# A re-ordered opening in a fused sliding-window attention and tanh-shrink layer

## The chip, the cores and the metric

The kernel runs on one core of one Trainium2 chip. The metric is the device time of one launch in microseconds (us), the median of three runs. Engine names are those of the profile: PE (TensorE matmuls), PEld (its weight loads), DVE (VectorE), ACT (ScalarE), POOL (GpSimd) and SP (SyncE, which here only issues transfers).

## The reference

Eight batches of eight heads, 576 tokens of 64 numbers. Each token attends to itself and the 63 tokens before it. The result, 4608 tokens of 512 numbers, goes through two matrix products with a tanh shrink between them.

```python
scores = scale * np.matmul(q, k.transpose(0, 1, 3, 2))
mask = (rel >= 0) & (rel < 64)              # rel = query position - key position
scores = np.where(mask, scores, -1e9)
attn = np.exp(scores - scores.max(-1, keepdims=True)); attn /= attn.sum(-1, keepdims=True)
x = np.matmul(attn, v).transpose(0, 2, 1, 3).reshape(4608, 512)
h = x @ w_in                                # 512 -> 2048
out = (h - np.tanh(h)) @ w_out              # 2048 -> 512
```

## The kernel before

The whole program is a list of some 1170 short words, `PLAN`, that `play` reads from left to right. Each word issues a handful of instructions, and every engine runs its own instructions strictly in the order of the list; between engines semaphores hold an instruction back until its operands are ready. So the list alone sets who is queued behind whom, on each engine and on the two queues that issue transfers, POOL's and SP's.

Attention goes by *pairs* of heads (four pairs in a batch, so pair 9 is the second of batch 2). The words for a pair g, with the engine:

- `lk`/`lq` load k and q (POOL, which casts float32 to bfloat16 on the way; the two with `.s` go through SP in float32). `ck`/`cq` re-arrange the loaded rows on the engine named by the last letter (p POOL, a ACT, v DVE). The first pairs are transposed without that step.
- `Ep`/`Fp` transpose q and k on PE, `Ec`/`Fc` copy the result out of PSUM (ACT or DVE).
- `Rp` computes the scores of half a pair on PE, `Rx` the exponentials on ACT. For pairs 0 to 3 the mask is added by a matmul of `hide`; from pair 4 on DVE multiplies by a mask (`M`).
- `LV.b.i` loads one tile of 128 tokens of v of batch b, `lv` and `lt` parts of batch 1; `zr`, `za`, `zb`, `Z` copy v to the other half of the partitions. A pair's product with v needs all five tiles of its batch and their copies.
- `P` (pairs 0 to 3) and `PP` (two pairs at once) compute probabilities times v on PE; `D`, `DS`+`DH` and `DR`+`DN` divide by the row sums on DVE. P.0, P.1 and P.3 use the same two PSUM banks, so each waits for the division of the one before.
- `Xp` transposes the attention result on PE, `Xc` copies it into a chunk of 512 tokens (`xT`).

The layers go by chunks c of 512 tokens and blocks m of 128 of the 2048 hidden numbers: `H.c.m` is four matmuls of 512 columns with w_in, `Hp.c.m.half` two of them, for one half of the input (half 0 comes from the first two pairs of the batch). `A` is the tanh on ACT, `G` the subtraction on DVE; for the first two chunks the results rotate through three PSUM banks. `W.c.s.part` is four matmuls with the part-th quarter of w_out, `O` copies the finished 128 tokens out of PSUM and SP stores them. `wi` and `wo` load the five blocks of w_in and the four of w_out. `U.n.bank` issues n matmuls of a constant tile whose result nobody reads.

From batch 3 on, rows of k and q are loaded by token (`lr`, `qr`) and transposed by SP's transfers (`tk`, `tq`); `S` computes the scores of two pairs there and needs all of the batch's transposed q and k.

Two rules of the queues matter below. POOL works in order, its own copies (`cq.4.p` and the like) and fills among its transfers, and its transfers rotate through eight semaphores, so that one is issued only when the eighth before it has landed. SP issues transposing transfers and the stores of the output from one queue.

Of the kernel before, what the change touches and what calls it, by code (L numbers as in the profile page):

```python
# [15 lines left out]
def kernel(  # L16
# [9 lines left out]
    nc = tc.nc  # L26
    B, H, S, D = q.shape
    NP = H // 2
    NJ = S // 64
    E, P = 6, S // 6  # L30
# [7 lines left out]
    M = d_ff // 128  # L38
# [162 lines left out]
    def make_ident():  # L201
        nc.gpsimd.memset(ident, 0.0)
# [312 lines left out]
    def subtract(c, m, s=None):  # L515
# [3 lines left out]
        i=make_ident, u=make_warm, mv=pads_v, mt=pads_k, mk=pads_kw, mz=pads_q8, tz=tail_q, U=warm_up, h=make_hide, n=make_mask, N=put_mask,  # L519
# [12 lines left out]
    def play(script):  # L532
# [5 lines left out]
        u mv.0 mv.1 lk.1.p lq.2.p LV.0.2 U.1.3 U.1.3 U.1.5 U.1.7 U.1.6 lk.3.p U.1.1 U.1.7 lk.2.p U.1.7 lq.1.p  # L538
        lq.3.p U.4.3 LV.0.0 i lk.0.s lq.0.s U.1.3 U.1.2 U.4.0 LV.0.3 U.4.0 Ep.2.3 Fp.1.5 U.1.2 Ec.2.3.v zr.0.2.v
        Fc.1.5.a ck.0.a mt.3 mt.1 U.1.1 U.1.3 U.1.2 U.1.4 mt.2 U.1.1 U.1.4 cq.0.a Fp.0.1 Fp.2.6 Ep.0.2 LV.0.1  # L540
        Ep.1.3 U.1.7 Fp.3.5 Fc.2.6.a LV.0.4 lk.4.p lq.4.p h Ec.0.2.a Fc.3.5.a Ep.3.7 Ec.3.7.a Ec.1.3.v mt.0
        Fc.0.1.v Rp.1.0.3 lk.5.p Rp.3.0.1 Rx.1.0.3 Rp.0.1.5 zr.0.3.v Rx.3.0.1 zr.0.0.v zr.0.1.v Rp.1.1.4
        Rp.3.1.0 ck.4.v Rx.0.1.5 Rx.1.1.4 Rx.3.1.0 lq.5.p Rp.0.0.2 wi.1 wi.0 lq.6.p P.1 lv.1.1.0 lk.7.p D.1
        Rx.0.0.2 cq.4.v Rp.2.1.0 Rp.2.0.3 Rx.2.1.0 P.0 Rx.2.0.3 P.2 Fp.4.2 ck.5.a Fc.4.2.a D.0 Ep.4.4 DS.2 P.3
        U.1.3 lk.6.p DH.2.0 Ec.4.4.a wi.2 Xp.0.0.1.2 Fp.5.0 Xp.0.0.0.3 D.3 lv.1.0.1 lk.8.p lq.7.p U.1.4 DH.2.1
        Xc.0.0.0.3.v Rp.4.1.5 U.1.1 lv.1.1.1 Xc.0.0.1.2.v Xp.0.1.0.7 cq.5.a Xp.0.1.1.1 Ep.5.3 Fc.5.0.a
        Xc.0.1.1.1.v Rx.4.1.5 Hp.0.0.0 mz Xc.0.1.0.7.a ck.7.a Ec.5.3.v Hp.0.2.1 Hp.0.0.1 Rp.4.0.6 Rp.5.1.3 n
        Hp.0.1.0 U.1.5 Hp.0.2.0 Hp.0.1.1 cq.6.v ck.6.v A.0.0 Ep.6.5 Rx.5.1.3 Rx.4.0.6 G.0.0 lv.1.0.0 A.0.2 A.0.1
        G.0.2 wi.3 H.0.3 A.0.3 G.0.1 N U.1.7 G.0.3 lq.8.p Fp.6.3 cq.7.v Fp.7.7 Ec.6.5.a H.0.4 ck.8.a H.0.6
# [101 lines left out]
```

## Time and profile before

| | us |
|---|---|
| median of three runs | 307.73 (307.4 to 307.78) |
| the profiled execution, first to last instruction | 305.2 |
| PE busy | 297.8 |
| the first layer's first matmul starts (Hp.0.0.0) | 22.58 |
| first matmul of W.2.0.1, from where both plans are alike | 109.08 |

The profiled execution's own span is 305.2 us; 2.5 us of the median lie outside it. Times in the profile count from the first instruction. A row of the timeline gives the start, the duration, the engine, the line of the kernel, the operation with its operands, and how often it stands there in a row; in brackets stands how long the engine was idle before it, and what ended the wait. A matmul's row ends some 0.2 us after the next matmul may start, so paces are read from start to start.

### The profile page before, as it was taken

What the parts mean: (1) busy time and instruction counts of PE and PEld (TensorE: products, weight loads), DVE (VectorE), ACT (ScalarE), POOL (GpSimd) and SP (SyncE); (2) the same over time, 40 slices, a digit from 0 to 9 for tenths busy, and PEclk for the clock granted to TensorE, in tenths of its full rate; (3) what the DMA queues carried; (4) which work ended last, traced back from release to release, by engine and by line L of the source; (5) the groups of instructions that cost most, each with busy time, mean ns of one, the idle gap of its engine ahead of it and who ended that gap; (6) DMA issues with size and microseconds to landing.
All of it is one profiled execution on the core that took longest, in us unless ns stands there. A gap on an engine that the chain in (4) does not pass through costs nothing.

```text
span 305.2 us, 6469 instructions
## 1 busy us (share of the span) xinstructions
PE 297.8 (98%) x2599; PEld 149.4 (49%) x2632; DVE 176.2 (58%) x316; ACT 157.5 (52%) x265; POOL 103.7 (34%) x141
## 2 busy tenths in 40 slices
PE   8999999999999999999999999999999999999995
PEld 3574555545455545444544444444544444444443
DVE  1687993289577745675387475657673645355300
ACT  1898975487565346534564645345633433433211
POOL 8989775800994290019005770000000000000000
PEclk9999999999999999999999999999999999999999
DMA  9999999995999999949999999560143010001112
GB/s 155 159 195 193 195 207 180 159 205 102 102 143 127 173 125 181 182 108 131 164 177 127 135 173 142 95 143 35 37 76 74 0 69 37 34 34 37 52 51 104
DMA packets 132878, 36.77 MB, mean 120 GB/s; under 512 B 119920, under 2 KB 127344, under 8 KB 132848
## 3 DMA queue, kind: packets, MB, share of 16 engines
q0 software_dynamic: 92752, 18.06, 85.3%
q1 hardware_dynamic: 40096, 18.30, 31.5%
q8 instruction: 20, 0.33, 0.5%
q14 instruction: 10, 0.08, 0.1%
HBM read 36.70 MB, written 9.44 MB: 151 GB/s over the span
## 4 chain that ended last, share of the span: by engine, by line
PE 87%; DVE 5%; ACT 3%; issue 2%; POOL 2%; DVEq 0%; ACTq 0%; POOLq 0%
PE ps L474 38%; PE ps L431 30%; PE ps L508 6%; PE ps L348 3%; PE ps L304 2%; DVE gT L445 2%; PE ps L397 1%; ACT th L439 1%; PE ps L286 1%; PE ps L467 1%; DVE pt L323 1%; PE ps L260 1%; PE ps L281 1%; PE ps L227 1%; POOL qall L110 1%
## 5 line engine op out<-in xcount | busy, mean ns | idle before, releaser
L445 DVE TENSOR_TENSOR gT<-ps,th 128x512 bf16<-128x512 f32 x144 | 97.2, 687 | 85.3 <-ACT th L439 84.6
L474 PE MATMUL ps<-w_out_sb,gT 128*128 128x512 bf16 x527 | 131.5, 380 | 2.2 <-issue 0.8
L439 ACT ACTIVATE th<-ps 128x512 f32<-128x512 f32 x144 | 84.7, 599 | 93.0 <-PE ps L431 79.7
L431 PE MATMUL ps<-xT,wi 128*128 128x512 bf16 x496 | 120.7, 380 | 0.1
L474 PEld LDWEIGHTS <-gT 128*128 128x128 bf16 x560 | 53.3, 98 | 61.4
L431 PEld LDWEIGHTS <-wi 128*128 128x128 bf16 x496 | 47.0, 98 | 54.3
L145 POOL DMA_DIRECT2D vw<-in_v_dram x35 | 30.0, 872 | 36.1 <-PE ps L348 33.5
L90 ACT ACTIVATE ysb<-ps 128x512 f32<-128x512 f32 (+1 forms) x24 | 14.2, 593 | 30.9 <-PE ps L474 30.2
L166 POOL DMA_DIRECT2D qall<-in_q_dram x25 | 21.7, 881 | 24.1 <-DMA qw<-qall 21.4
L166 POOL DMA_DIRECT2D kall<-in_k_dram x25 | 21.7, 875 | 10.4 <-DMA kw<-kall 4.8
L314 ACT ACTIVATE pt<-ps 128x1024 bf16<-128x1024 f32 (+1 forms) x30 | 23.3, 816 | 3.5 <-PE ps L304 3.2
L323 DVE TENSOR_TENSOR pt<-pt,ps 128x1152 bf16<-128x1152 bf16 x28 | 20.5, 749 | 5.1 <-ACT pt L314 3.2
L508 PE MATMUL ps<-xT,wi 128*128 128x512 bf16 x80 | 20.8, 380 | 0.0
L92 DVE COPY ysb<-ps 128x512 f32<-128x512 f32 (+1 forms) x11 | 7.1, 650 | 20.5 <-PE ps L467 13.2
L368 DVE TENSOR_TENSOR xs<-ps,rcp 128x384 bf16<-128x384 f32 x28 | 15.2, 550 | 0.3
L318 ACT ACTIVATE pt<-ps 128x640 bf16<-128x640 f32 (+1 forms) x24 | 14.7, 659 | 0.8 <-PE ps L286 0.8
L348 PEld LDWEIGHTS <-pt 128*64 128x64 bf16 x504 | 9.4, 112 | 6.3 <-DVE pt L323 2.1
L90 ACT ACTIVATE kt<-ps 128x576 bf16<-128x576 bf16 x10 | 6.5, 647 | 10.8 <-PE ps L256 6.8
L227 PE MATMUL ps<-warm 128*128 128x512 bf16 (+1 forms) x35 | 10.6, 435 | 1.1 <-DVE warm L207 1.1
L508 PEld LDWEIGHTS <-wi 128*128 128x128 bf16 x80 | 7.4, 98 | 8.5 <-issue 0.4
L348 PE MATMUL ps<-vw,pt 128*64 128x65 bf16 x504 | 11.0, 197 | 0.3 <-DVE pt L323 0.2
L365 DVE TENSOR_TENSOR xs<-ps,rcp 128x384 bf16<-128x384 f32 x14 | 7.7, 550 | 0.1
(74 smaller groups left out, 166.7 us busy)
## 6 DMA issues: line engine op xcount, KB each, us to landing
out_dram<-ysb SPq DMA_DIRECT2D x33, 256.0 KB, 3.1
vw<-in_v_dram POOLq DMA_DIRECT2D x28, 128.0 KB, 6.6
qall<-in_q_dram POOLq DMA_DIRECT2D x20, 128.0 KB, 7.5
kall<-in_k_dram POOLq DMA_DIRECT2D x20, 128.0 KB, 6.8
w_out_sb<-in_moe_w_out_dram POOLq DMA_DIRECT2D x4, 512.0 KB, 8.2
kall<-in_k_dram POOLq DMA_DIRECT2D x11, 144.0 KB, 6.3
qall<-in_q_dram POOLq DMA_DIRECT2D x11, 144.0 KB, 6.6
wi<-in_moe_w_in_dram POOLq DMA_DIRECT2D x3, 512.0 KB, 7.9
```

Of the source, the lines that this page charges most:

```text
L90: nc.scalar.activation(o, i, ACT.Copy)
L145: nc.gpsimd.dma_start(out=w[:, 2 * i + 1, :, 0:D] if i < NF else w[64:128, 2 * i, :, 0:D], in_=v[b, :, 128 * i:128 * i + n].rearrange("h p ...
L166: nc.gpsimd.dma_start(out=token_rows(b, n)[0:c, i], in_=(q if n == "q" else k)[b, :, 128 * i:128 * i + c].rearrange("h p d -> p h d"))
L314: nc.scalar.activation(o, sp, ACT.Exp, scale=scale)
L323: nc.vector.tensor_tensor(p, p, mask.unsqueeze(1).to_broadcast([128, 2 * NJ, 64]), ALU.mult)
L348: nc.tensor.matmul(ps[r, bank, 65 * i:65 * i + 65], PT[(g + r2) % NPT][:, j, r], vw[b % 2][:, j, p0 + r2 + NP * h, :], start=True, stop=True)
L368: nc.vector.tensor_tensor(xs[b % 2][:, p0 // 2, 0:6, n // 2, :], ov[:, :, 0:D], sums[g][:, n].to_broadcast([128, 6, D]), ALU.mult)
L431: nc.tensor.matmul(hp, w_in_tile(ki, m), chunk_tile(c)[:, n.start // 64:n.stop // 64, ki % 2, 64 * (ki // 2):64 * (ki // 2) + 64], start=( ...
L439: nc.scalar.activation(th[:, n], hp, ACT.Tanh)
L445: nc.vector.tensor_tensor(gT[c][:, m, columns(s)], hp, th, ALU.subtract)
L474: nc.tensor.matmul(yp, gT[c][:, m, s * 128:(s + 1) * 128], w_out_sb[:, m, :], start=n == 1 and i == 0, stop=n == 4 and i == 3)
L508: nc.tensor.matmul(hp, w_in_tile(half + 2 * i, m), chunk_tile(c)[:, :, half, 64 * i:64 * i + 64], start=n == 1 and i == 0, stop=n == 2 and ...
```

## The change

Three things change in the code, and the first 550 words of the plan (570 before); the last 604 words are the same.

- The three constant tiles `ident`, `hide` and `seen` are filled by DVE in a new word `iv`; POOL keeps only the selects.
- Copies out of PSUM, casts and copies of v change engines here and there: k of pair 0 is cast by DVE (`ck.0.v`), q of pair 4 and k of pairs 5, 8 and 9 by POOL (`cq.4.p`, `ck.5.p`, `ck.9.p`, `ck.8.p`).
- The order: q of pairs 2, 0 and 1 is transposed first; three of w_out's four blocks are issued close together; k and q of batch 2 are loaded behind w_out, and batch 3's loads and transposes stand in one piece. There are 30 matmuls of the constant tile in place of 35.

```diff
     def make_ident():
-        nc.gpsimd.memset(ident, 0.0)
         nc.gpsimd.affine_select(ident, ident, compare_op=ALU.not_equal, fill=1.0,
                                 base=0, pattern=[[-1, 128]], channel_multiplier=1)
+
+    def fill_masks():
+        nc.vector.memset(ident, 0.0)
+        nc.vector.memset(hide, 0.0)
+        nc.vector.memset(seen, 1.0)
...
     def make_hide():
-        nc.gpsimd.memset(hide, 0.0)
...
     def make_mask():
-        nc.gpsimd.memset(seen, 1.0)
...
-        u mv.0 mv.1 lk.1.p lq.2.p LV.0.2 U.1.3 U.1.3 U.1.5 U.1.7 U.1.6 lk.3.p U.1.1 U.1.7 lk.2.p U.1.7 lq.1.p
-        lq.3.p U.4.3 LV.0.0 i lk.0.s lq.0.s U.1.3 U.1.2 U.4.0 LV.0.3 U.4.0 Ep.2.3 Fp.1.5 U.1.2 Ec.2.3.v zr.0.2.v
...
+        u U.8.3 U.7.4 U.7.2 mv.0 lk.1.p lq.1.p mv.1 lq.0.s cq.0.a lk.0.s mt.0 iv ck.0.v mt.2 lq.2.p LV.0.3 i
+        lk.2.p LV.0.0 lk.3.p LV.0.1 LV.0.2 lk.6.p lq.3.p h LV.0.4 lq.6.p lk.4.p lq.5.p lk.5.p lq.4.p n wi.1 wi.0
+        Ep.2.2 Ep.0.0 Ec.0.0.a Ep.1.1 Ec.1.1.a Ec.2.2.a Fp.0.4 Fp.1.5 U.4.7 Fp.2.3 Fc.1.5.a Fc.0.4.v Rp.0.0.6
...
```

**POOL's first transfers.** `vw_85` is v of batch 0, `kall`/`qall` with 102 and 104 are batch 0 and with 103 and 105 batch 1. Before:

```order
L110 DMA kall_104<-in_k_dram 96x2x384
L110 DMA qall_102<-in_q_dram 96x2x384
L145 DMA vw_85<-in_v_dram 128x8x64
L110 DMA kall_104<-in_k_dram 96x2x384 x2
L110 DMA qall_102<-in_q_dram 96x2x384 x2
L145 DMA vw_85<-in_v_dram 128x8x64
L202 MEMSET ident 128x128
L203 ISA
L203 AFFINE_SELECT ident<-ident 128x128
L145 DMA vw_85<-in_v_dram 128x8x64 x2
L145 DMA vw_85<-in_v_dram 64x8x64
```

Now:

```order
L110 DMA kall_104<-in_k_dram 96x2x384
L110 DMA qall_102<-in_q_dram 96x2x384 x2
L145 DMA vw_85<-in_v_dram 128x8x64
L202 ISA
L202 AFFINE_SELECT ident<-ident 128x128
L110 DMA kall_104<-in_k_dram 96x2x384
L145 DMA vw_85<-in_v_dram 128x8x64
L110 DMA kall_104<-in_k_dram 96x2x384
L145 DMA vw_85<-in_v_dram 128x8x64 x2
L110 DMA kall_105<-in_k_dram 96x2x384
L110 DMA qall_102<-in_q_dram 96x2x384
L234 AFFINE_SELECT hide<-hide 128x128
```

The q of pair 2 goes from second to third place, the q of pair 3 (the last `qall_102`) from seventh to eleventh, and the last, shorter tile of v (64x8x64) from eleventh to twelfth, behind the selects of `hide`.

**ACT ahead of the first layer.** `pt` are exponentials (`Rx`), `qp`/`kt` copied transposes, `xT` the chunks, `th` the tanh. Before, from the sixth of the eight exponentials of pairs 0 to 3 on:

```order
L318 ACTIVATE pt<-ps 128x640
L318 ACTIVATE pt<-ps 128x512
L318 ACTIVATE pt<-ps 128x640
L90 ACTIVATE kb_111<-kall_105 96x2x6x64
L90 ACTIVATE kt_88<-ps 128x576
L90 ACTIVATE qp_94<-ps 128x576
L90 ACTIVATE qb_108<-qall_103 96x2x6x64
L90 ACTIVATE kt_89<-ps 128x576
L318 ACTIVATE pt<-ps 128x512
L90 ACTIVATE xT_112<-ps 128x4x128
L90 ACTIVATE kb_110<-kall_105 96x2x6x64
L439 ACTIVATE th<-ps 128x512
```

Now, from the fifth on:

```order
L320 ACTIVATE pt<-ps 128x512
L90 ACTIVATE qp_97<-ps 128x576
L320 ACTIVATE pt<-ps 128x640 x2
L90 ACTIVATE qb_108<-qall_103 96x2x6x64
L320 ACTIVATE pt<-ps 128x512
L90 ACTIVATE kt_88<-ps 128x576
L90 ACTIVATE xT_112<-ps 128x4x128
L90 ACTIVATE xT_113<-ps 128x128
L90 ACTIVATE qp_96<-ps 128x576
L90 ACTIVATE xT_112<-ps 128x4x128 x2
L90 ACTIVATE xT_113<-ps 128x128
L90 ACTIVATE qp_95<-ps 128x576
```

The cast of pair 5's q (`qb_108`) now stands before the last exponential of pair 3 (the `pt` of 512), and three of the four `Xc` are ACT's.

**SP ahead of batch 4's scores.** `kw_92` and `qw_98` are the transposed k and q of batch 4. Before:

```order
L171 DMA_TRANSPOSE kw_92<-kall_104 128x4x64
L495 DMA out_dram<-ysb 128x512 x2
L171 DMA_TRANSPOSE kw_92<-kall_104 128x4x128
L179 DMA_TRANSPOSE qw_98<-qall_102 128x4x128
L171 DMA_TRANSPOSE kw_92<-kall_104 128x4x128 x2
L179 DMA_TRANSPOSE qw_98<-qall_102 128x4x64
L179 DMA_TRANSPOSE qw_98<-qall_102 128x4x128
L171 DMA_TRANSPOSE kw_92<-kall_104 128x4x128
L179 DMA_TRANSPOSE qw_98<-qall_102 128x4x128 x2
```

Now:

```order
L497 DMA out_dram<-ysb 128x512 x3
L179 DMA_TRANSPOSE qw_98<-qall_102 128x4x128 x2
L171 DMA_TRANSPOSE kw_92<-kall_104 128x4x64
L179 DMA_TRANSPOSE qw_98<-qall_102 128x4x128 x2
L171 DMA_TRANSPOSE kw_92<-kall_104 128x4x128 x3
L179 DMA_TRANSPOSE qw_98<-qall_102 128x4x64
L171 DMA_TRANSPOSE kw_92<-kall_104 128x4x128
```

All ten transposes of batch 4 now stand behind the store of O.1.2; before, one stood ahead of the stores of O.1.0 and O.1.1, and nine between these and the store of O.1.2.

More of the change, by code (lines that the diff above doesn't have):

```diff
@@ new lines @@
+        Hp.2.1.0 A.2.1 O.1.1.v G.2.1 H.2.4 A.2.4 G.2.4 Z.3 S.12 Sx.12.0 Sx.12.2 Sx.12.1 H.2.5 H.2.2 W.1.2.0
+        W.1.2.2 M.12 M.13 A.2.5 A.2.2 PP.12 G.2.2 G.2.5 H.2.10 H.2.7 W.1.2.1 W.1.2.3 A.2.10 A.2.7 DR.12 DN.12.2
+        DN.12.1 G.2.7 DN.12.0 O.1.2.v G.2.10 H.2.9 S.14 A.2.9 H.2.8 Sx.14.0 Sx.14.2 A.2.8 Sx.14.1 G.2.9 G.2.8
+        M.15 M.14 LV.4.3 lr.5.2 qr.5.4 qr.4.4 lr.4.0 LV.4.4 qr.5.3 LV.4.0 lr.5.0 tq.4.2 tq.4.1 tk.4.4 tq.4.0
+        tq.4.3 tk.4.1 tk.4.2 tk.4.3 tq.4.4 tk.4.0 H.2.11 A.2.11 W.1.3.3 W.1.3.1 H.2.12 PP.14 G.2.11 DR.14
@@ new lines @@
+        A.3.13 LV.5.1 LV.5.2 lr.6.1 qr.6.1 A.3.14 G.3.13 W.3.0.2 H.3.15 tz.5.v G.3.14 qr.6.3 H.3.12 W.3.0.0
+        A.3.15 G.3.15 Hp.4.1.0 A.3.12 G.3.12 Hp.4.1.1 A.4.1 W.3.0.1 G.4.1 W.3.0.3 Hp.4.0.1 H.4.3 Hp.4.0.0
+        O.3.0.v tk.6.3 tk.6.2 A.4.0 S.20 A.4.3 Sx.20.2 Sx.20.0 Sx.20.1 tq.6.0 tk.6.0 W.3.1.1 G.4.0 G.4.3 W.3.1.0
+        H.4.2 W.3.1.3 A.4.2 S.22 G.4.2 H.4.4 W.3.1.2 H.4.7 A.4.4 G.4.4 M.20 O.3.1.a Sx.22.0 Sx.22.1 A.4.7
+        W.3.2.1 H.4.6 W.3.2.2 A.4.6 Sx.22.2 W.3.2.3 Z.5 G.4.7 M.22 M.21 H.4.9 PP.20 G.4.6 tq.7.1 tq.6.1 A.4.9
@@ L621 @@
+        H.8.10 A.8.10 G.8.5 G.8.10 W.7.1.3 H.8.9 H.8.8 A.8.9 O.7.1.v A.8.8 W.7.2.3 W.7.2.2 G.8.9 G.8.8 H.8.12
+        H.8.13 A.8.12 A.8.13 W.7.2.1 W.7.2.0 G.8.12 G.8.13 H.8.11 O.7.2.a H.8.14 W.7.3.1 A.8.11 A.8.14 G.8.11
+        H.8.15 W.7.3.3 W.7.3.2 W.7.3.0 A.8.15 G.8.15 G.8.14 W.8.0.3 W.8.0.1 W.8.0.0 O.7.3.v W.8.3.3 W.8.1.3
+        W.8.0.2 W.8.1.2 O.8.0.a W.8.2.2 W.8.1.1 W.8.1.0 W.8.2.3 W.8.2.0 W.8.2.1 O.8.1.a W.8.3.2 O.8.2.a O.9.0.a
+        W.8.3.0 W.8.3.1 O.8.3.v"""
     play(PLAN)
```

147 lines of the change are left out of this document (65 added, 82 removed).

## The prediction

> **What bounds the kernel now.** I read the page first, then PE's busy time by stage, then the timelines of the first 23 us engine by engine.
>
> ```profile
> span 305.2 us, 6469 instructions
> PE 297.8 (98%) x2599; PEld 149.4 (49%) x2632; DVE 176.2 (58%) x316; ACT 157.5 (52%) x265; POOL 103.7 (34%) x141
> PE 87%; DVE 5%; ACT 3%; issue 2%; POOL 2%; DVEq 0%; ACTq 0%; POOLq 0%
> ...
> 0.00:22.58 22.58, 21.07 (x336) 12.42 (x337) 12.17 (x35) 14.43 (x23) 19.50 (x35) 1.00 1.46 169
> 22.58:41.12 18.54, 18.52 (x207) 9.48 (x205) 16.01 (x34) 16.48 (x31) 14.17 (x23) 1.00 1.44 196
> ...
> 90.14:109.08 18.94, 18.59 (x191) 9.77 (x194) 14.37 (x26) 8.09 (x14) 9.73 (x13) 1.00 2.03 145
> ```
>
> PE bounds it: 98% busy, 87% of the chain of waits. The stage rows (stretch, length, then PE, PEld, DVE, ACT, POOL busy, the granted clock, DMA) show that behind 22.58, where the first layer starts, PE is idle for 0.02 us of the next 18.5 and 0.35 of the last 19 before 109. Little is to be had there. What can be gained lies ahead of the first layer, where PE is busy largely with matmuls of the constant tile:
>
> ```profile
> 1.06 6.54 PE L227 MATMUL ps<-warm 128*128 128x512 bf16 x22 [1.06 <-DVE warm L207]
> 7.70 0.45 PE L256 MATMUL ps<-ident,qall 96*64 96x96 bf16 x12
> ...
> 12.46 0.45 PE L281 MATMUL ps<-hide,ident 128*128 128x320 bf16 x2
> ...
> 13.13 0.43 PE L281 MATMUL ps<-hide,ident 128*128 128x320 bf16 x2
> ...
> 16.06 0.51 PE L335 MATMUL ps<-vw,pt 128*64 128x65 bf16 x20
> ...
> 17.81 0.51 PE L335 MATMUL ps<-vw,pt 128*64 128x65 bf16 x20
> ...
> 19.59 0.51 PE L335 MATMUL ps<-vw,pt 128*64 128x65 bf16 x20
> ...
> 22.58 1.54 PE L508 MATMUL ps<-xT,wi 128*128 128x512 bf16 x6
> ...
> 109.08 1.03 PE L474 MATMUL ps<-w_out_sb,gT 128*128 128x512 bf16 x4
> ```
>
> The opening is a chain: load, transpose (7.70), scores (half a pair every 0.67 from 12.46 to 13.13), P.1 (16.06), P.0 (17.81), P.3 (19.59), the division, Xp and Xc, Hp.0.0.0 (22.58). From 109.08 (W.2.0.1) both plans are word for word the same, so **the change is worth the difference in when PE reaches W.2.0.1**, unless a queue arrives there in another state.
>
> Counted by words, PE does the same between the first layer's start and W.2.0.1 in both plans (40 H, 16 Hp, 32 W, six PP, eleven Xp, two S and the scores), but for two things: one group of six transposes more stands ahead of the first layer now, and two single constant matmuls, of 512 and 384 columns, that stood behind it are gone. So the new time of W.2.0.1 is the new start of the first layer, plus the old 86.50 us (109.08 - 22.58), less these two, plus or minus waits.
>
> **The change part by part.** First the loads, since the new chain hangs on them.
>
> ```profile
> 1.36 0.76 POOL L110 DMA_DIRECT2D kall<-in_k_dram  x1 [0.84 <-POOLq L635]
> 2.12 0.65 POOL L110 DMA_DIRECT2D qall<-in_q_dram  x1
> 2.75 0.91 POOL L145 DMA_DIRECT2D vw<-in_v_dram  x1
> ...
> 4.90 1.29 POOL L110 DMA_DIRECT2D qall<-in_q_dram  x2
> ...
> 7.02 0.27 POOL L202 MEMSET ident<- 128x128 bf16 x1
> ...
> qall<-in_q_dram POOLq DMA_DIRECT2D x2, 144.0 KB, 5.4
> ...
> qall<-in_q_dram POOLq DMA_DIRECT2D x2, 144.0 KB, 5.7
> ...
> 13.30 1.41 DVE L92 COPY vw<-vw 64x520 bf16<-64x520 bf16 x4 [0.22 <-DMA vw<-in_v_dram]
> 15.04 0.59 DVE L92 COPY vw<-vw 64x520 bf16<-64x520 bf16 x2 [0.33 <-DMA vw<-in_v_dram]
> ```
>
> The two qall rows are transfers in windows 2 to 5 and 5 to 8 us; their last column is issue to landing. In the second place q landed at 2.12 + 5.4 = 7.5; pair 3's q, seventh, at 5.54 + 5.7 = 11.2; the last full tile of v, tenth, when DVE's wait ends at 15.04. From 11.2 to 15.0 three tiles of v landed, 1.25 us each; between 7.5 and 11.2 one tile and four k or q, so some 0.6 us each for these. By these paces q of pair 2, now third, lands at 8.1 to 8.5 (not 7.5); then tile, k, tile, k, two tiles, k, q: **pair 3's q at 15.5** (11.2 before) and the last, half tile of v at 16.1. The fills that POOL gives up save 0.27 us ahead of this, about what `hide`'s selects now cost ahead of the half tile; on DVE they lie in its idle time before the first copy. I take 0 for them; without that cover they cost the same 0.3.
>
> Step 1, the first transposes: at 8.4 in place of 7.70. The 22 constant matmuls end at 7.6 as before, so PE idles 0.8 us; nothing on the chain waits for it, because step 2 comes later.
>
> Step 2, products with v. The half tile (16.1) sets P.0: the copies of the other tiles (0.59 each) are done by 15.6, pair 3's q is transposed from 15.5 to 15.9. P.0 starts at 16.2 (P.1 before: 16.06). The next product on these banks follows 1.75 later (17.81 - 16.06), as the division needs: P.1 at 17.95.
>
> Step 3, P.3. Prices:
>
> ```profile
> 16.68 0.22 DVE L375 RECIPROCAL rc<-ps 128x10 f32<-128x10 f32 x1 [0.56 <-PE ps L335]
> 16.94 0.82 DVE L377 TENSOR_TENSOR xs<-ps,rc 128x640 bf16<-128x640 f32 x1
> ...
> 13.37 3.50 ACT L318 ACTIVATE pt<-ps 128x640 bf16<-128x640 f32 x6
> ...
> 20.52 0.84 ACT L90 ACTIVATE qb<-qall 96x768 bf16<-96x768 bf16 x1
> ...
> 22.26 0.60 ACT L90 ACTIVATE xT<-ps 128x512 bf16<-128x512 bf16 x1
> ```
>
> Behind P.0 (some 0.45) PE does two halves of scores (0.67 each), pair 2's and pair 3's, to 18.0; pair 3's other half stands behind P.1 (18.4 to 19.1). ACT meanwhile does pair 3's first exponential (from 18.05, 3.50/6 = 0.6), then the cast of pair 5's q (0.84) and only then the last exponential (0.6): 18.05 + 2.05 = 20.1. P.3 starts at 20.1, against 19.59: **+0.5**.
>
> Step 4, into the first layer. P.3 to its division 0.62 (16.68 - 16.06), reciprocal and product 1.1, the last half division 0.4 (half of 0.82), nine transposes on PE 0.5, the last copy on ACT 0.6, and some 0.15 for hand-overs: 20.1 + 3.3 = **23.4 for H.0.3**. The old plan began at 22.58 with Hp.0.0.0, which needs the first two pairs alone; H.0.3 needs all four. So **+0.82**.
>
> Step 5, what was moved ahead of it.
>
> ```profile
> 60.04 0.42 PE L260 MATMUL ps<-ident,kb 96*128 96x96 bf16 x6
> 60.30 0.42 PE L260 MATMUL ps<-ident,qb 96*128 96x96 bf16 x6
> ...
> 285.44 5.18 PE ps L474 x24
> ```
>
> A group of six transposes is 0.26 (60.30 - 60.04). A matmul of 512 columns is 5.18/24 = 0.216, one of 384 three quarters of it, 0.16; the two constant matmuls are 0.38. **-0.64** together. The other constant matmuls stand where PE waits anyway, in both plans.
>
> Step 6, waits behind the start. One goes: DVE copied batch 2's v just ahead of PP.8,
>
> ```profile
> 63.30 2.75 PE L431 MATMUL ps<-xT,wi 128*128 128x512 bf16 x12
> ...
> 65.36 0.71 DVE vw L152
> 66.11 0.76 PE ps L348 x34
> ```
>
> so that PE began it at 66.11 and not at 63.30 + 12 x 0.216 = 65.89. That copy (`Z.2`) now stands some 6 us of PE's work ahead of PP.8: **-0.2**. Others come. A first-layer block holds its PSUM bank for 1.03 on PE (109.08's row has the same four matmuls), about 0.6 on ACT and 0.7 on DVE, 2.35 in all; three banks at 0.864 give 2.59. Each of the seven exponentials (0.6) of this stage exceeds the 0.24 of slack by 0.36, and a group of scores or half a block on PE hides most of it: between 0 and 2.5 in all. I take **+0.55**, near the lower end, because the old plan, with seven such exponentials there too, shows 0.02 us of idle PE in that stage.
>
> The w_in blocks are issued from 15.0 to 18.0 and the fifth behind POOL's cast of pair 4's q. Nearest row for that cast:
>
> ```profile
> 30.73 0.64 POOL L92 COPY vw<-vw 64x520 bf16<-64x520 bf16 x1
> ...
> wi<-in_moe_w_in_dram POOLq DMA_DIRECT2D x1, 512.0 KB, 8.2
> ```
>
> 768 columns by that pace are 0.95. Pair 4's q, fifth behind the half tile, lands at 16.1 + 5 x 0.6 = 19.1, so the cast ends at 20.1, wanted by PE at 22.8. The fifth block lands at 20.1 + 0.8 + 8.2 = 29.1, or 31 behind three others, wanted at 33. The cover is 2 us in both. The w_out blocks stand close together, but the last lands some 2.4 us earlier than before, since two k and two q were put behind it (4 x 0.6). Batch 2's eight k and q and a tile of v then take 8 x 0.6 + 1.25 = 6 us, while PE has ten W (8.6 us) between the first use of that block and the transposes of pairs 10 and 11. These I cost at nothing; without the cover each transfer late is a wait of 0.6 or 1.25.
>
> The sum: +0.82 - 0.64 - 0.2 + 0.55 = **+0.53**, against the profiled span 305.2: 305.7. With the 2.5 us by which the median exceeds the span (307.73 - 305.2), **308.2**.
>
> **The rivals.**
>
> *The opening isn't late.* If the last tile, half as long, lands at 15.3 and P.3's exponential isn't held up, the first layer starts at 22.9; and if the first-layer stage runs like the old one, the 0.55 goes too: +0.3 - 0.64 - 0.2 = -0.5, and without the visible idle time of the last stage row (0.35) -0.9: **306.8**. For it: PE's waits behind 22.58 are few in the old plan, and w_in comes earlier. Against it: four more transfers stand ahead of pair 3's q.
>
> *Casts at the head of in-order engines.* Pair 5's q, third behind the half tile, lands at 17.9 and is wanted by ACT at 18.65; pair 4's k, second, at 17.3, and is wanted by DVE at 17.9. If the loads run 1.5 us late (the three tiles took 1.25 each, a w_in block 8.2 to land), both casts hold up everything behind them: ACT's exponential, DVE's second division. From 0.7 us of lateness on, each further us goes into P.3, and the wait spreads to the first layer's tanh: the forecast's 0.5, 0.8 more in P.3 and 0.7 in the tanh make +2.0, **309.7**.
>
> *The clock.* The rows above show 1.00 granted throughout, also from 7.70 on, where the old plan put seven constant matmuls between the transposes. The new plan has 0.8 us of idle PE there, then transposes with one group of constant matmuls of 384 columns. If the clock fell to half there, the eight groups of scores (0.67 each by 5.4 us in all) would take up to 5.4 more, half of it in the shadow of the loads: +2.7, **310.9**. The Trainium skill, "TensorE: Matmul & The Clock Gate", Part 4, says that transposes don't count as activity for the gate as other matmuls do, and Part 1 that an idle window brings half the clock; by that rule this case would come about, and the trace of before can't tell, having constant matmuls among them.
>
> *Batch 4's transposes.*
>
> ```profile
> 107.15 2.61 SPq L179 DMA_TRANSPOSE qw<-qall  x2
> ...
> 116.27 0.22 PE L299 MATMUL ps<-q,kw 128*128 128x64 bf16 x2
> ...
> kw<-kall SPq DMA_TRANSPOSE x25, 3.9
> ```
>
> SP takes 1.3 each. All ten now stand behind O.1.2's store, at about 98: the last is issued by 111 and lands 3.9 later, at 115, with batch 4's scores due at 116. If the store comes 2 us later, PE waits 1: **309.2**.
>
> *The change does little:* head and waits cancel, **307.7**.
>
> **How the numbers follow.** The forecast 0.37, opening not late 0.27, casts 0.16, clock 0.08, batch 4 0.07, nothing 0.05. About 0.2%, 0.6 us, is what a measurement of this kernel can tell from no change. The forecast's own range is 307.3 to 309.1; of its 0.37 I put 0.17 within 0.2%, 0.17 slower, 0.03 faster. Faster: 0.27 + 0.03 = 0.30. Within 0.2%: 0.17 + 0.05 = 0.22. Slower: 0.17 + 0.16 + 0.08 + 0.07 = 0.48. The range reaches to 306.0 (the first rival, with 0.8 us more) and to 310.8 (the casts with a us more, just short of the clock).
>
> **What would show it.** In the new profile: first transposes at 8.4 (step 1); DVE or PE waiting for vw at 16.1 (step 2); P.3 at 20.1 with ACT's cast right ahead of the last exponential (step 3); H.0.3 at 23.4 (step 4); W.2.0.1 at 109.5. A first layer before 22.9 or after 24.5, a clock below 1.00 in the first 20 us, or PE waiting for wi, w_out or kw/qw would make it wrong.

## The result, and the profile after

The change is slower: 309.17 us (median of 20 runs, 307.74 to 310.13) against 307.92 (20 runs, 307.35 to 309.64), a ratio of 1.0034 with a 95% interval of 1.0019 to 1.0049 (not the quotient of the two medians, which is 1.0041). The forecast was 308.2. The direction is right; the next sections show that a queue which the sum left out has a large part in it.

The page of the changed kernel, with the stage rows of its timeline (stretch, length, then PE, PEld, DVE, ACT, POOL busy, granted clock, DMA):

```profile
span 306.8 us, 6489 instructions
PE 300.0 (98%) x2627; PEld 148.9 (49%) x2627; DVE 182.4 (59%) x323; ACT 150.9 (49%) x256; POOL 107.1 (35%) x143
PE 81%; DMA 9%; POOL 5%; DVE 2%; issue 1%; ACT 1%; SPq 0%; DVEq 0%; POOLq 0%; ACTq 0%
...
0.00:22.80 22.80, 21.14 (x338) 12.19 (x339) 12.94 (x37) 14.57 (x25) 20.87 (x36) 1.00 1.30 164
22.80:41.99 19.19, 18.42 (x187) 8.81 (x187) 13.94 (x25) 14.63 (x28) 12.84 (x20) 1.00 1.35 185
91.01:109.95 18.94, 18.81 (x194) 9.71 (x193) 16.02 (x27) 9.29 (x18) 3.81 (x5) 1.00 1.17 120
```

PE is as busy as before by share, but transfers now have 9% of the chain of waits, where before they had no entry. The stage behind the first layer's start, which had 0.02 us of idle PE, has 0.77. PE's rows that answer to those of the prediction, and all its later waits that the timeline shows:

```profile
1.06 6.57 PE L231 MATMUL ps<-warm 128*128 128x512 bf16 x22 [1.06 <-DVE warm L211]
8.04 0.45 PE L258 MATMUL ps<-ident,qall 96*64 96x96 bf16 x12 [0.40 <-DMA qall<-in_q_dram]
...
15.63 0.49 PE L337 MATMUL ps<-vw,pt 128*64 128x65 bf16 x20
...
19.53 0.51 PE L337 MATMUL ps<-vw,pt 128*64 128x65 bf16 x20
...
22.80 1.02 PE L433 MATMUL ps<-xT,wi 128*128 128x512 bf16 x4
24.53 0.61 PE L510 MATMUL ps<-xT,wi 128*128 128x512 bf16 x2 [0.70 <-DMA wi<-in_moe_w_in_dram]
...
67.57 0.76 PE L350 MATMUL ps<-vw,pt 128*64 128x65 bf16 x36 [0.21 <-DVE qp L92]
68.78 2.87 PE L433 MATMUL ps<-xT,wi 128*128 128x512 bf16 x12 [0.20 <-DVE gT L447]
...
109.95 1.03 PE L476 MATMUL ps<-w_out_sb,gT 128*128 128x512 bf16 x4
...
143.86 0.59 PE L510 MATMUL ps<-xT,wi 128*128 128x512 bf16 x2 [0.44 <-DMA xT<-xs]
```

The first layer starts at 22.80 (22.58 before), W.2.0.1 at 109.95 (109.08). So 0.87 of the 1.6 us between the two profiled spans is there when the common words begin. The other 0.7 comes behind it, in words that are the same in both plans. The wait at 143.86 is Hp.4.1.1's, for the second half of chunk 4's input, which SP's transposing transfers `Y.4.1` bring. The two queues behind it, SP's first, of the kernel before:

```profile
95.58 1.00 SPq L495 DMA_DIRECT2D out_dram<-ysb  x2
96.67 1.31 SPq L171 DMA_TRANSPOSE kw<-kall  x1
...
105.93 3.52 POOL L166 DMA_DIRECT2D kall<-in_k_dram  x4 [4.29 <-DMA qw<-qall]
...
120.90 2.53 SPq L171 DMA_TRANSPOSE kw<-kall  x2
...
135.51 0.53 SPq L495 DMA_DIRECT2D out_dram<-ysb  x1
136.13 2.62 SPq L416 DMA_TRANSPOSE xT<-xs  x2
```

and of the change:

```profile
88.94 10.45 SPq L497 DMA_DIRECT2D out_dram<-ysb  x2
99.48 2.92 SPq L179 DMA_TRANSPOSE qw<-qall  x2
...
112.03 0.88 POOL L166 DMA_DIRECT2D kall<-in_k_dram  x1 [17.21 <-DMA kw<-kall]
...
121.83 3.13 SPq L171 DMA_TRANSPOSE kw<-kall  x2
...
138.09 0.53 SPq L497 DMA_DIRECT2D out_dram<-ysb  x1
138.71 2.63 SPq L418 DMA_TRANSPOSE xT<-xs  x2
```

SP stood from about 89 to 99.4 at the store of O.1.2, which waited for its PE and DVE work, with batch 4's ten transposes queued behind it. The load at the head of POOL's queue, a k tile of batch 6, goes into rows that those transposes read, and loads of batch 5 are queued behind it: POOL stood 17.21 us until 112.03 instead of going on by 105.93. SP's next transposes, of batch 5, read those loads, and the transposes of x stand behind them: they issue at 138.71 in place of 136.13. From the first transposes of batch 5 behind the join (tk.5.2) to those of x, in words that are the same in both plans, SP takes 16.88 us (121.83 to 138.71) in place of 15.23 (120.90 to 136.13). That the late loads cause this is shown only in part: in this execution one of these transposes waits 0.9 us for a load of q, and for SP's other waits the profile names no load. The chain of waits of the change, in order of time, shows the last steps:

```profile
137.61 0.70 DVE gT L447
138.32 0.30 SPq L497
...
138.71 5.11 DMA xT<-xs
143.82 0.04 issue
143.86 0.59 PE ps L510 x2
```

It leads back over the store of O.2.2 (138.32) to DVE, not over POOL's loads, because this store ended SP's last wait; SP had worked off its transposes at 138.00 and stood 0.3 us for the store.

### The profile page after: what moved, and what is told of

Its sections match the earlier page's. It is cut to its first block, busy times and chain, and to the rows that moved or that the text cites. A ratio compares the mean times of both kernels' runs of the same rounds, so it can differ in the third digit from the quotient of the medians.

```text
span 306.8 us, 6489 instructions
## 1 busy us (share of the span) xinstructions
PE 300.0 (98%) x2627; PEld 148.9 (49%) x2627; DVE 182.4 (59%) x323; ACT 150.9 (49%) x256; POOL 107.1 (35%) x143
## 4 chain that ended last, share of the span: by engine, by line
PE 81%; DMA 9%; POOL 5%; DVE 2%; issue 1%; ACT 1%; SPq 0%; DVEq 0%; POOLq 0%; ACTq 0%
PE ps L476 38%; PE ps L433 30%; PE ps L510 5%; DMA wi<-in_moe_w_in_dram 4%; PE ps L350 3%; DMA vw<-in_v_dram 2%; PE ps L306 2%; DMA xT<-xs 2%; DMA qall<-in_q_dram 1%; PE ps L469 1%; PE ps L399 1%; POOL vw L132 1%; POOL vw L145 1%; POOL vw L92 1%; POOL w_out_sb L198 1%
## 5 line engine op out<-in xcount | busy, mean ns | idle before, releaser
L476 PE MATMUL ps<-w_out_sb,gT 128*128 128x512 bf16 x560 | 134.9, 379 | 0.0
L145 POOL DMA_DIRECT2D vw<-in_v_dram x35 | 30.3, 875 | 20.1 <-PE ps L350 16.9
L90 ACT ACTIVATE ysb<-ps 128x512 f32<-128x512 f32 (+1 forms) x20 | 11.8, 592 | 28.4 <-PE ps L476 27.7
L92 DVE COPY ysb<-ps 128x512 f32<-128x512 f32 (+1 forms) x15 | 9.9, 657 | 18.8 <-PE ps L469 13.2
L370 DVE TENSOR_TENSOR xs<-ps,rcp 128x384 bf16<-128x384 f32 x28 | 15.1, 551 | 0.3
L90 ACT ACTIVATE xT<-ps 128x512 bf16<-128x512 bf16 (+3 forms) x15 | 6.6, 491 | 7.7 <-PE ps L399 7.6
L231 PE MATMUL ps<-warm 128*128 128x512 bf16 (+1 forms) x30 | 8.4, 438 | 1.1 <-DVE warm L211 1.1
L92 DVE COPY kt<-ps 128x576 bf16<-128x576 bf16 x8 | 6.0, 749 | 5.2 <-PE ps L262 3.9
```

The source lines that it names most:

```text
L90: nc.scalar.activation(o, i, ACT.Copy)
L92: eng.tensor_copy(o, i)
L145: nc.gpsimd.dma_start(out=w[:, 2 * i + 1, :, 0:D] if i < NF else w[64:128, 2 * i, :, 0:D], in_=v[b, :, 128 * i:128 * i + n].rearrange("h p ...
L476: nc.tensor.matmul(yp, gT[c][:, m, s * 128:(s + 1) * 128], w_out_sb[:, m, :], start=n == 1 and i == 0, stop=n == 4 and i == 3)
```

## The experiments

The ratios are to the kernel before, run beside each kernel on the same chip. The first four kernels share one set of its runs, so do the next four (from the change again to the fills alone) and the last three; the fills' second run has its own.

**Two causes, and the converse.** The first kernel takes away the wait for w_in's block 0; block 4 of chunk 0 is put into the PSUM bank of block 1 before that block is subtracted there, so block 1 of chunk 0 holds other numbers.

```diff
- H.0.3 Hp.0.1.0 A.0.3 ... Hp.0.1.1 N Hp.0.2.0 Rx.6.0.5 A.0.1 G.0.1 Rp.4.0.5 Hp.0.2.1 Rx.4.0.5 A.0.2
+ H.0.3 Hp.0.2.0 A.0.3 ... Hp.0.2.1 N Hp.0.1.0 Rx.6.0.5 A.0.2 G.0.2 Rp.4.0.5 Hp.0.1.1 Rx.4.0.5 A.0.1
```

> The changed kernel, but its second first-layer half block is that of columns 512 to 767 of the first eighth group (Hp.0.2.0, which takes w_in's block 1, landed at 21.4) and the half block that takes w_in's block 0 (landed at 24.5) stands four groups later; no transfer moves. Theory A (0.87 us of the loss is PE's wait for block 0): PE does not wait for wi, W.2.0.1 starts at 109.1 to 109.3 in place of 109.95, ratio to the kernel before 1.0005 to 1.0015 in place of 1.0034. Rival (another chain, tanh or the DVE, takes the place of that wait): W.2.0.1 at 109.7 or later, ratio 1.003.

Measured: 310.17 us, ratio 1.009 (1.0057 to 1.0123). PE no longer waits for wi, yet W.2.0.1 starts at 110.17: a wait of 0.59 for DVE at 30.16 and one of 0.54 ahead of the first layer took the place. Behind the join the wait for x is larger than in the change itself:

```profile
145.48 0.59 PE L510 MATMUL ps<-xT,wi 128*128 128x512 bf16 x2 [1.90 <-DMA xT<-xs]
```

So theory A fails in this form, and the wait for x is not of one size: 0.44 in the change, 1.90 here, with SP's order the same.

The second kernel takes eight of the ten transposes out from behind the store. It is not the old order: the eight now stand together right behind O.1.1's store, and two stay behind O.1.2's.

```diff
- O.1.1.v G.2.1 ... O.1.2.v ... lr.5.0 tq.4.2 tq.4.1 tk.4.4 tq.4.0 tq.4.3 tk.4.1 tk.4.2 tk.4.3 tq.4.4 tk.4.0
+ O.1.1.v tq.4.2 tq.4.1 tk.4.4 tq.4.0 tq.4.3 tk.4.1 tk.4.2 tk.4.3 G.2.1 ... O.1.2.v ... lr.5.0 tq.4.4 tk.4.0
```

> The changed kernel, but eight of batch 4's ten transposes on SP stand ahead of O.1.2's store, as in the kernel before. Theory C (SP is held by that store until 99, so POOL's loads of batch 5 are released at 112 in place of 106 and the transposes of x come 2.6 us late): W.2.0.1 stays at 109.9, POOL's loads start by 106, the x transposes issue at about 136.5 in place of 138.71, PE's 0.44 us wait for xT at 143.9 goes, ratio 1.0015 to 1.0022 in place of 1.0034. Rival (SP only follows PE's 0.87 us): x transposes stay behind 138, ratio 1.003 to 1.004.

Measured: 307.58 us, ratio 0.9995 (0.9972 to 1.0018). POOL's load starts at 106.64, the transposes of x issue at 137.53, and PE waits nowhere behind 69 us. The edit gives back not half of the loss but all of it, as far as the interval tells.

Third, both edits (with the same block of other numbers):

> The two edits together. If both theories hold and the two losses add: W.2.0.1 at 109.1 to 109.3, no wait for xT, ratio 0.999 to 1.0005. If only one holds: 1.0010 to 1.0020. If neither: 1.0034.

Measured: 308.45 us, ratio 1.0018 (0.9999 to 1.0037). No wait for x, but the other block order costs again: 0.35 for w_in's block of 8 to 11 at 29.75 and 0.85 at PP.4 for POOL's copies of batch 1's v.

Fourth, the converse: the kernel before with batch 4's transposes behind the store, and with them three loads (`lr.6.4`, `lr.6.3`, `qr.6.0`) and two transposes of batch 5 that depend on them. So it moves a little more than those words.

```diff
- tk.4.4 ... tk.4.1 tq.4.0 tk.4.0 ... tk.4.3 tq.4.4 ... tq.4.3 tk.4.2 tq.4.1 ... tq.4.2 ... tk.5.4 ... tq.5.3 ... O.1.2.v PP.14
+ O.1.2.v tk.4.4 tk.4.1 tq.4.0 tk.4.0 tk.4.3 tq.4.4 lr.6.4 tq.4.3 tk.4.2 tq.4.1 lr.6.3 tq.4.2 tk.5.4 qr.6.0 tq.5.3 PP.14
```

> The kernel before, with batch 4's ten transposes and the three loads and two transposes that depend on them placed behind O.1.2's store, as the change has it; opening untouched. Theory C: x transposes issue 1.5 to 2.6 us later than 136.13, PE waits 0.3 to 0.6 us for xT or for kw/qw after 140, ratio 1.001 to 1.002. Rival (the store's place does not matter): 1.000.

Measured: 310.29 us, ratio 1.0082 (1.0053 to 1.0112), more than either theory said. In its profiled execution, its longest (313.97), PE reaches batch 4's scores before SP has brought the transposed q. PE's row, and PE busy and granted clock around it:

```profile
121.08 0.90 PE L304 MATMUL ps<-qw,kw 64*128 64x64 bf16 x26 [3.63 <-DMA qw<-qall]
...
117.00:119.00 2.00, 0.45 (x11) 1.00 2.21 158
119.00:121.00 2.00, 0.00 (x0) 0.61 4.77 48
121.00:123.00 2.00, 1.92 (x29) 0.50 1.48 218
123.00:125.00 2.00, 2.00 (x6) 0.50 0.42 161
125.00:127.00 2.00, 2.00 (x8) 0.69 0.00 0
```

The wait costs 3.63 and the half clock behind it 2.6 more (the two together are the 6.26 by which S.16 to S.18 is longer than before, in the table below). The median execution can't have lost that much, but the loss doesn't hang on the clock: the five of the nine runs at a mean clock of 1.00 took 309.03 to 310.29, all above the 307.82 of the kernel before. That is the stall which my fourth rival placed at 116. In quarters of a microsecond, the granted clock is 1.00 up to 119.25, 0.50 from 119.50 to 126.25 and 0.99 behind that, while PE's last matmul before the wait starts at about 117.4. So the clock fell some 2 us into the wait and came back some 5 us behind its end. The Trainium skill, "TensorE: Matmul & The Clock Gate", Part 1, says that an idle window of about 3.4 us halves the clock; this trace agrees that a wait of this size halves it, but here it took only those 2 us.

**The change again, and its other parts.** The changed kernel once more beside three others:

> The changed kernel once more, on the same chip as the three below. If the wait for the transposed x at 143.9 is what makes most of its loss (theory C), its profile shows that wait again, between 0.4 and 2 us, and the ratio to the kernel before is 1.002 to 1.005; if the wait was an accident of one execution, it is missing and the ratio is still 1.003.

Measured: 309.12 us, ratio 1.0056 (1.0036 to 1.0076). The profiled execution was its shortest (span 306.0, median of its runs 307.4) and still has the wait, 0.29 at 143.15.

Then two attempts on the first-layer stage, both with the transposes ahead of the store. One word: `Ec.11.3.v` becomes `Ec.11.3.a`.

> The changed kernel with batch 4's eight transposes ahead of the store, and pair 11's transposed q copied by ACT in place of DVE just ahead of PP.8. Theory B (DVE's backlog behind batch 2's v copy costs PE 0.21 and 0.20 us of visible waits at PP.8 and H.1.8, 0.65 in all counted in starts): both waits go, W.2.0.1 0.4 to 0.65 us earlier than with the transposes alone, ratio to the kernel before 0.9975 to 0.9985. Rival (ACT becomes late for the tanh instead): same as the transposes alone, 0.9995.

Measured: 308.03 us, ratio 1.0017 (1.0000 to 1.0033). PP.8 still waits 0.17, now by ACT's exponential, and H.1.8 0.20: theory B had the place but not what is late.

The block order again, with the blocks behind it moved so that each bank is free:

```diff
- H.0.3 Hp.0.1.0 ... Hp.0.2.0 ... H.0.6 A.0.6 H.0.4 ... H.0.8 Hp.0.0.1 ... H.0.7 ... H.0.5
+ H.0.3 Hp.0.2.0 ... Hp.0.1.0 ... H.0.6 A.0.6 H.0.5 ... H.0.7 Hp.0.0.1 ... H.0.8 ... H.0.4
```

> The changed kernel with batch 4's eight transposes ahead of the store, and chunk 0's hidden blocks in another order: 3, 2, 1, 6, 5, 7, 0, 8, 4 in place of 3, 1, 2, 6, 4, 8, 0, 7, 5, so that w_in's block 0 is wanted some 1.5 us later. Theory A (w_in's block 0, landing at 24.5, bounds the start of the first layer): no wait for wi, W.2.0.1 0.5 to 0.85 us earlier, ratio 0.997 to 0.998. Rival (the loads of q and v bound the opening just as late, as where the first layer began at 23.67 and did not wait): 0.999 to 1.000.

Measured: 308.5 us, ratio 1.0023 (1.0006 to 1.0040). No wait for wi; but 0.62 for DVE at 34.41 and 0.58 for POOL's copies of v at PP.4, and W.2.0.1 at 111.16. Avoiding the late block gains nothing in any of three tries.

Last, the fills alone, in the kernel before: `ident`, `hide` and `seen` filled by DVE right behind `mv.1`.

> The kernel before with one part of the change alone: ident, hide and seen are filled by DVE and no longer by POOL; its plan is as it was. My prediction costed this at 0: ratio 0.999 to 1.001, and POOL's loads issue 0.27 us earlier behind the fill of ident. Rival (the earlier loads or DVE's fills shift the opening): more than 0.3 us either way in the start of the first layer (22.58).

Measured: 308.35 us, ratio 1.0027 (1.0002 to 1.0053). POOL's selects on `ident` come 0.25 earlier, as forecast. But the profiled opening is 0.5 late from its first row on:

```profile
1.06 7.19 PE L231 MATMUL ps<-warm 128*128 128x512 bf16 x22 [1.06 <-DVE warm L211]
8.18 0.45 PE L258 MATMUL ps<-ident,qall 96*64 96x96 bf16 x12
```

The 22 constant matmuls took 7.19 us here and 6.54 in the execution of before. So that run could not say what the fills cost, and it was made once more:

> The kernel before with the fills alone on DVE, once more, since 1.0027 with an interval from 1.0002 to 1.0053 left open whether they cost anything. If they cost nothing (the constant matmuls at the start took 7.19 us in that execution and 6.54 in the one of before, and that alone moved the first transposes by 0.48): ratio 0.9990 to 1.0010, and first transposes within 0.1 us behind the end of the constant matmuls. If they cost 0.5 to 0.8 us: 1.0015 to 1.0030 again.

Measured: 308.22 us, ratio 1.0007 (0.9984 to 1.0029); the 22 matmuls took 6.51 and the transposes began at 7.52. The fills alone show no certain cost.

**Three more.** The transposes ahead of the store again:

> The changed kernel with batch 4's eight transposes ahead of O.1.2's store once more, to narrow its interval. If the rest of the change (opening, fills, first-layer stage) costs nothing in the median: ratio 0.9990 to 1.0005. If the rest costs the 0.3 to 0.6 us that the profiled executions show at batch 4's first scores: 1.001 to 1.002. No wait for xT in either case, and 22.3 us between the scores at 124 and those at 146.

Measured: 307.78 us, ratio 0.9996 (0.9983 to 1.0008). W.2.0.1 starts at 110.33 in its profiled execution, later than in the change's own, and the stretch from 125.15 to 147.46 is 22.31 us, without a wait.

The store itself moved off SP's queue, the transposes left where the change has them:

```diff
-        nc.sync.dma_start(out=out[r0:r0 + 128, :], in_=ysb)
+        queue = nc.scalar if (c, s) == (1, 2) else nc.sync
+        queue.dma_start(out=out[r0:r0 + 128, :], in_=ysb)
```

> The changed kernel with one edit: the store of chunk 1's third block (O.1.2) is issued from ACT's queue; SP's ten transposes keep their place in the plan, but no longer stand behind a store. Theory C, in its narrow form (it is the store at the head of SP's in-order queue): SP's transposes start when their rows have landed, at about 89, no wait for xT, 22.3 us between the scores at 124 and at 146, ratio 0.999 to 1.002 (ACT may be held up to 1 us by the copy that the store waits for). Rival (the transposes' later place itself, or the loads): the wait for xT stays, 22.8 us or more, ratio 1.003 to 1.006.

Measured: 308.91 us, ratio 1.0025 (1.0008 to 1.0041). SP's transposes start at 89.89, and from batch 4's second scores to batch 5's first is 22.32 us with no wait for x: the narrow theory holds. The total is another matter: ACT was idle for 3.46 us around the store, which it issued at 100.82, and PE, short of a tanh, waited 1.22 at 102.62. My "up to 1 us" for ACT was too low. With a late opening in that execution besides (first layer at 24.37), W.2.0.1 came at 111.91.

Last, the attempt to beat both, on top of the transposes ahead of the store:

```diff
- Rx.8.1.5 A.1.3 ... H.1.6 Ec.11.3.v Rx.10.1.4 A.1.5 PP.8
+ Rx.8.1.5 Rx.10.1.4 A.1.3 ... H.1.6 Ec.11.3.a A.1.5 PP.8
```

> An attempt to beat both: the transposes ahead of the store, pair 11's transposed q copied by ACT, and pair 10's first exponential in ACT's order right behind pair 8's, where ACT was idle, so that PP.8 no longer waits for its bank. If PP.8's wait came from that exponential: PP.8 starts 0.2 to 0.4 us earlier against the matmuls ahead of it and the wait at H.1.8 (0.20) goes too, ratio to the transposes alone 0.998 to 0.999. If DVE's masks set PP.8: no change.

Measured: 307.13 us, ratio 0.9966 (0.9948 to 0.9983), below the kernel before. PE's and ACT's rows of the transposes ahead of the store alone (the eighth run):

```profile
63.81 3.67 PE L433 MATMUL ps<-xT,wi 128*128 128x512 bf16 x16
67.75 0.76 PE L350 MATMUL ps<-vw,pt 128*64 128x65 bf16 x36 [0.27 <-DVE qp L92]
68.44 0.32 PE L288 MATMUL ps<-qp,kt 64*128 64x64 bf16 x10
68.96 2.22 PE L433 MATMUL ps<-xT,wi 128*128 128x512 bf16 x9 [0.20 <-DVE gT L447]
...
67.10 0.60 ACT L320 ACTIVATE pt<-ps 128x512 bf16<-128x512 f32 x1 [1.56 <-DVE pt L325]
```

and of this kernel:

```profile
63.87 3.67 PE L433 MATMUL ps<-xT,wi 128*128 128x512 bf16 x16
67.47 0.76 PE L350 MATMUL ps<-vw,pt 128*64 128x65 bf16 x36
68.16 0.32 PE L288 MATMUL ps<-qp,kt 64*128 64x64 bf16 x10
68.42 2.77 PE L433 MATMUL ps<-xT,wi 128*128 128x512 bf16 x12
...
63.93 1.08 ACT L320 ACTIVATE pt<-ps 128x512 bf16<-128x512 f32 x2
```

In the first, pair 10's exponential waits 1.56 us for DVE's mask, and PP.8's row names DVE although the bank that it needs is only free behind that exponential. In the second, it runs at once with pair 8's, PP.8 starts 3.60 us behind its block row in place of 3.94, and H.1.8's wait is gone as well, together 0.6 us. Without the exponential's move (`Ec.11.3.a` alone, above) the copy's move gained nothing that showed; the exponential's move without the copy's was not run.

## Why the prediction was right or wrong

The same words put side by side, from the profiled executions (us). S.16 and S.18 are batch 4's scores, S.20 is batch 5's first; all starts are rows of PE.

| kernel | first layer | W.2.0.1 | S.16 to S.18 | S.18 to S.20 |
|---|---|---|---|---|
| before | 22.58 | 109.08 | 7.63 | 22.32 |
| fills alone, first and second run | 23.07, 22.39 | 109.36, 108.85 | 7.84, 7.78 | 22.61, 22.75 |
| before, transposes late | 23.44 | 109.82 | 13.89 | 22.55 |
| the change, first and second run | 22.80, 23.32 | 109.95, 109.45 | 7.63, 7.64 | 22.91, 22.76 |
| other block order, first try | 23.05 | 110.17 | 7.63 | 24.38 |
| transposes ahead, first and second run | 23.67, 22.71 | 109.88, 110.33 | 7.63, 7.63 | 22.32, 22.31 |
| store on ACT's queue | 24.37 | 111.91 | 7.63 | 22.32 |
| exponential early | 23.39 | 109.44 | 7.63 | 22.32 |

**The step that failed** is the one on which the sum stands: "the change is worth the difference in when PE reaches W.2.0.1, unless a queue arrives there in another state". I named the exception and then priced the sum without it. SP's queue did arrive in another state. From tk.5.2 to the transposes of x, in the same words, SP takes 16.5 to 18.3 us in the three executions with the change's order, and 14.4 to 15.8 in the other eleven. (One of these is the old plan with the transposes late, 14.7; there PE had stalled just before, which gave the loads more time.) In the changed plan with its own order the last column is 22.76 to 24.38; with the transposes ahead, or with the store on ACT's queue, it is 22.3 to 22.4 in all seven executions (three of them not in the table), also with a W.2.0.1 of 111.91. In medians, taking the transposes out from behind the store is worth 0.4 to 0.6%: 1.0034 and 1.0056 with the change's order, 0.9995 and 0.9996 without, and the spans' medians say the same (307.4 for the change, 305.9 and 306.1 without, 305.8 to 306.1 for the kernel before on the same chips).

Two things stay open. The some 1.4 us between those spans are more than the wait for x in the change's two profiled executions (0.44 and 0.29), both shorter than its median run; the 1.90 of the other block order, profiled at its median, shows that the wait can be that large. And the old order is no clean base: in the two runs of the old plan with the fills alone, 0.5 and 0.6 us are lost from S.16 to S.20 as well, though not for x. There ACT's copy of O.2.1 waits 1.5 us (in the second run the profile names a store's landing, in the first PE), and PE then waits for DVE. So the transposes right behind O.1.1 may be better than both orders; the old plan with them there was not run.

**The fourth rival**, batch 4's transposes, had this cause, the words and the store, at a chance of 0.07 and at 309.2. Its place was wrong for the change: the last transpose of batch 4 was issued at 111.62 (111 in the prediction) and landed 3.8 later, before the scores at 117.20, and PE waited only 19 us behind S.18, for x. In the kernel before with the transposes late, the wait came where the rival had put it, in its longest execution. That its 309.2 meets the measured 309.17 is luck: it was 1 us for another wait, on top of 0.53 that the medians do not show.

**Step 1** gave 8.4 for the first transposes: 8.04, and between 7.50 and 8.41 in other executions of this opening. What I had not seen is that the constant matmuls ahead of them end between 7.5 and 8.6 from one execution to the next, in both plans.

**Step 2** gave a wait for the last half tile of v until 16.2. In the first profile there is none (P.0 at 15.63); in the second PE waits 0.77 for vw until 16.49, and in three others with this opening 0.37, 0.59 and 0.95. So the cause is there in four of ten executions, and the step called it certain.

**Step 3**, the cast of pair 5's q in front of the last exponential, is there,

```profile
18.02 0.83 ACT L90 ACTIVATE qb<-qall 96x768 bf16<-96x768 bf16 x1
18.76 0.58 ACT L320 ACTIVATE pt<-ps 128x512 bf16<-128x512 f32 x1
```

and P.3 comes at 19.53 (20.1 forecast) or, in the second run, at 20.15.

**Step 4** gave 23.4 for the first layer, +0.82. Ten executions have the change's words up to there (the changed kernel's two and the eight others made from it); their mean is 23.38, between 22.71 and 24.37. So the time was right. The old opening has a mean of 22.87 in four executions (22.58, 23.07, 22.39, 23.44), so the 22.58 that I started from was early and the difference is +0.5. The rival "the opening is not late" has 22.9, and two of the ten are that early.

**Steps 5 and 6** gave -0.64 - 0.2 + 0.55 = -0.29 between the first layer and W.2.0.1. Four executions have the change's words throughout that stretch, but for the place of batch 4's transposes in two of them (22.80, 23.32, 23.67 and 22.71): 86.78 on average, against 86.41 in the four of the old plan, +0.37. Since -0.64 is a count of work, the waits, which I put at 0.55 - 0.2 = 0.35, are about 1.0. The 0.2 at PP.8 did not go: PE waits there as long, now for DVE's copy of a transposed q. The visible part is at three places: PP.8 and H.1.8 (0.4 to 0.5 in each execution), w_in's block 0 (0.70 in one of four), which I had costed "at nothing" with a cover of 2 us that was worked out for its fifth block, and POOL's copies of batch 1's v ahead of PP.4 (0.77 in one of four). The two executions that start early (22.80, 22.71) are those with these last two waits, so there the early start was given back. In these same eight executions W.2.0.1 comes 0.62 later, against +0.53 forecast: the sum came near, with too much in the opening and too little in the waits behind it.

**Why this +0.6 isn't in the medians.** With the transposes ahead of the store, the kernel is level with before. Two things may give it back. The time outside the span is 1.7 us in the median of every kernel with the new opening and 1.8 to 2.0 with the old one. And the old order of SP's queue is itself not free, as the two runs with only the fills changed show. That plain executions of before do so too, on average, would fit their median span, 0.6 to 0.9 over the profiled 305.2; no profile shows it, so this half is argued.

**The clock rival** fell: the granted clock is 1.00 in every stage row of the change, and a group of four constant matmuls of 384 columns among the transposes ran at full pace (0.82 us; at half the pace four would take 1.3). The Trainium skill's "TensorE: Matmul & The Clock Gate", Part 4, says that transposes do not count as activity in the same way; these some 3 us of mostly transposes (8.04 to 11.02), with those four matmuls among them, show no loss of clock, and a longer stretch was not run. **The casts rival** was not seen in the change's own two executions; the nearest to it is the run with the store on ACT's queue, where v's half tile came at 17.37, P.3 at 21.03 and the first layer at 24.37.

**Sizes.** The forecast's base, 2.5 us outside the span, set a median beside another execution's span. Measured run by run it is 1.7 to 1.9, and the profiled 305.2 was a short execution.

## What to carry to other kernels

When a re-ordered plan joins the old one, compare more than the time at which the busiest engine arrives: for each queue that serves several consumers, write down what it has issued by then and what it stands at. A store that waits for compute, placed ahead of independent transfers in one in-order queue, delays them by its whole wait, and the price may come up 40 us later, as a wait for something else. Undo such an order as an experiment, and check that what you put in its place is really the old one. And where the profile names one engine as the releaser of a wait, look for idle time on the engine that has to free the buffer: moving pair 10's exponential into such a gap, together with one copy moved to ACT, gained 0.3%, of which the rows show 0.6 us.

## What the runs showed of the hardware

- A wait of 3.63 us on PE cost 2.6 us more. The clock was granted at 0.50 from some 2 us into the wait (119.5) until some 5 us behind its end (126.25). Four of the nine runs of that kernel have a mean clock of 0.989 to 0.995, and these are its longest, 310.95 to 313.97; no run of the kernel before, of 30 beside it, is under 0.998.
- The opening's 22 constant matmuls took between 6.43 and 7.57 us from one execution to the next (14 executions, both openings), and the transposes behind them move by as much. At the later pace of 0.216 they would be 4.75. The granted clock is shown as 1.00 throughout that time, so this column does not tell the slow start.
- In the change's first profile w_in's five blocks were issued within 4.1 us (before, within 13.7). Block 0 landed 8.2 us after its issue and the fifth block 12.1; before, 6.5 and 7.9.
- The store on ACT's queue was issued at 100.82, though DVE's copy that it reads ended at 99.60. The profile names the landing of one of SP's transposed k as what ended ACT's wait.
